# Attention weights of batch 2 through the DMA crossbar, and the second softmax half of batches 4 to 7 one slice earlier

## The chip, the cores and the metric

One core of one Trainium2 chip. The metric is the device time of the whole program in microseconds (us). Small effects are read from the traces, from a fixed matmul on, and the times are a check on the sum.

## The reference

Eight batches of a cross attention between 512 tokens and 32 state rows per head (8 heads of 64), both ways, followed by a gated feed-forward network on the 8 x 544 rows.

```python
def _attn_ref(x, state):                       # x [8,8,512,64], state [8,8,32,64]
    scores = scale * np.matmul(x, state.transpose(0, 1, 3, 2))
    a = np.exp(scores - scores.max(-1, keepdims=True)); a /= a.sum(-1, keepdims=True) + 1e-09
    xread = np.matmul(a, state)
    ...                                        # a2: softmax over the tokens, the other way round
    sread = np.matmul(a2, x)
    return np.concatenate([xread, sread], axis=2)

def _moe_ref(x, w_gate, w_val, w_out):         # [4352,512], 512 -> 1536 -> 512
    return (np.maximum(x @ w_gate, 0.0) * (x @ w_val)) @ w_out
```

## The kernel before

The kernel never forms `xread`. It multiplies each batch's state with the weights once (`U`, matmuls `up`), so that gate and value are `a` times `U` (matmuls `gv_ps<-ans,U`). For that the attention weights `a_sn`, which the softmax leaves with tokens on the partitions, have to be transposed to `ans`. In the kernel before this is done by TensorE for batches 0, 1 and 2, and by the DMA crossbar for batches 3 to 7.

```python
    def att_aT_dma(b):                                   # crossbar
        ans_alloc(b)
        nc.sync.dma_start_transpose(out=ANS[b].rearrange("p k c t -> p (k c) t"),
                                    in_=a_sn[b].rearrange("p k c m -> p (k c m)"))

    def att_T(b, kc):                                    # TensorE: 4 transposes into one PSUM bank
        ...
        for c in range(NC):
            nc.tensor.transpose(ps[:, c], a_sn[b][:, kc, c], id128)
        held["aT", b, kc] = ps

    def att_out(b, kc, eng):                             # and a copy out of PSUM
        copy[eng](out=ANS[b][:, kc], in_=held["aT", b, kc])
```

The part up to batch 2 is a hand-written list of steps (`aT.2.1@4` is `att_T(2, 1)` in PSUM bank 4, `ao` is `att_out`). From there on a loop runs over slices: one slice is a group of four `gv` matmuls, its relu on ScalarE, its product on VectorE, and a group of four `o_ps` matmuls for a slice 18 earlier. Twelve slices make a batch, and work for the next batch is hung on fixed slices:

```python
    for b in range(3, B):
        s = b - 1                                        # work for batch b in the slices of batch b-1
        for i, jf in enumerate((4, 5) if b == 3 else (3, 5)):
            at(s, jf, att_half, b, i)                    # scores, exp (ScalarE), sum, reciprocal, scaling (VectorE)
        for part, jf in enumerate((7, 10)):
            at(s, jf, u_block, b, part)                  # three groups of 8 up matmuls, six PSUM banks
        if b + 1 < B:
            at(s, 9, x_next, b + 1)                      # cast of x on GpSimd, then crossbar transpose xT
            at(s, 9, x_pad, b + 1)                       # copy xa on GpSimd
        if b + 2 < B:
            at(s, 10, x_dma, b + 2, (nc.sync,))          # 1 MB load of x
    for b in range(B):
        s, jf = {0: (2, 3), 1: (2, 4), 2: (2, 7), 3: (2, 10)}.get(b, (b - 1, 10))
        if b > 1:
            at(s, jf, sr, b)
        at(s, jf + 1, sr_T_dma, b)                       # crossbar transpose of sn
        at(s, jf + 6, sr_out, b, "act")                  # copy br on ScalarE, waits for it
    ...
    for g in range(first, NF * (B + 1)):                 # cut
        gv(b, jf); relu(b, jf); mult(b, jf)
        out_piece(...)
        for f in units.get(g, ()):
            f()
```

Six PSUM banks go round among `gv_ps` (two per slice), scores (one) and `up` (two per group). All transfers that the change touches are issued by SyncE, from one queue, in program order.

The softmax here doesn't subtract the row's maximum and nothing guards it: scores larger than these inputs give would overflow.

## Time and profile before

| | kernel before |
|---|---|
| time, median of three runs | 223.29 us (222.69 to 223.47) |
| span of the profiled execution | 221.3 us |
| start of the last store, which ends the chain of waits | 216.40 us |
| start of the up block of batch 4 to the gv group after it | 88.88 - 86.48 = 2.40 us |
| the same for batches 5, 6, 7 | 1.70 to 1.71 us |

An up block is three groups of `up` matmuls followed by four `o_ps` matmuls; the next `gv` start is used as its end, because in some traces the record of the first `o_ps` matmul is missing.

One more view matters: the transfers in SyncE's queue, with start, duration of the issue, and what is moved.

```profile
73.10 1.81 SPq L168 DMA_TRANSPOSE xT<-xb  x1
75.01 1.10 SPq L105 DMA_DIRECT2D xf<-in_x_dram  x1
76.20 0.59 SPq L377 DMA_DIRECT2D out_dram<-o_sb  x1
76.88 1.45 SPq L286 DMA_TRANSPOSE hs_sb<-sn  x1
```

The small transpose of `sn` is issued 1.9 us after a 1 MB load, and lands 1.2 us after it (82.80 and 81.61 us in the trace).

### The profile page before, as it was taken

The page shows a single profiled execution, that of the slowest core. Times are in us where ns is not written, and L with a number is a line of the kernel's source. Part 1 is how long each engine was busy: PE and PEld are TensorE (multiplying, and loading weights), DVE is VectorE, ACT ScalarE, POOL GpSimd, SP SyncE. Part 2 cuts the span into 40 slices and gives each one's busy share as a digit, 9 for nine tenths or more (in the row PEclk, how much of TensorE's full clock was granted, in tenths as well). Part 3 has the DMA queues.
Part 4 walks back from the last instruction along what each step waited for, and adds up shares of the span by engine and source line. Part 5 has one row for each costly group of instructions (what it writes and reads, how often), then busy time and mean ns, then how long its engine had stood idle before and what let it go on. Part 6 is the DMA issues. An engine that isn't in the chain of part 4 may idle for free.

```text
span 221.3 us, 4871 instructions
## 1 busy us (share of the span) xinstructions
PE 216.4 (98%) x1955; PEld 105.9 (48%) x1955; DVE 129.9 (59%) x229; ACT 125.1 (57%) x238; POOL 48.6 (22%) x54
## 2 busy tenths in 40 slices
PE   7899999999999999999999999999999999999994
PEld 3554455444544453444444444445444445666544
DVE  2697898965787558564767378646875333222100
ACT  5599887565667547465565456645654544222222
POOL 8777845460001524006000700000000000000000
PEclk9999999999999999999999999999999999999999
DMA  7999999172058582691169113511311112211132
GB/s 154 174 194 196 199 241 277 49 192 77 16 116 241 110 275 78 141 264 52 49 146 280 58 47 95 110 41 50 96 50 53 49 47 47 52 56 71 66 95 95
DMA packets 40343, 26.01 MB, mean 118 GB/s; under 512 B 21536, under 2 KB 35744, under 8 KB 40320
## 3 DMA queue, kind: packets, MB, share of 16 engines
q1 hardware_dynamic: 27456, 17.47, 28.4%
q0 software_dynamic: 11968, 7.47, 21.9%
q10 hardware_dynamic: 896, 0.75, 1.3%
q8 instruction: 15, 0.25, 0.5%
q14 instruction: 8, 0.07, 0.1%
HBM read 18.35 MB, written 8.91 MB: 123 GB/s over the span
## 4 chain that ended last, share of the span: by engine, by line
PE 88%; DMA 7%; DVE 1%; ACT 1%; POOL 1%; issue 1%; DVEq 0%; POOLq 0%; ACTq 0%
PE o_ps L365 37%; PE gv_ps L328 36%; PE gv_ps L345 5%; PE up L303 4%; DMA xb<-in_x_dram 3%; DMA hs_sb<-sn 3%; PE upc L303 2%; PE sc_ps L209 1%; PE sr_ps L273 1%; DMA out_dram<-o_sb 1%; PE xT_ps L195 1%; PE aT_ps L244 1%; DVE h_sb L356 1%; ACT o_sb L373 1%; POOL xb L427 0%
## 5 line engine op out<-in xcount | busy, mean ns | idle before, releaser
L365 PE MATMUL o_ps<-wo_sb,h_sb 128*128 128x512 bf16 x372 | 94.8, 379 | 0.0
L328 PE MATMUL gv_ps<-ans,U 128*128 128x512 bf16 x384 | 94.0, 379 | 0.0
L356 DVE TENSOR_TENSOR h_sb<-gv_ps,g_sb 128x512 bf16<-128x512 f32 x96 | 65.1, 689 | 44.1 <-ACT g_sb L352 42.2
L352 ACT ACTIVATE g_sb<-gv_ps 128x512 bf16<-128x512 f32 (+1 forms) x108 | 62.5, 581 | 45.2 <-PE gv_ps L328 34.4
L328 PEld LDWEIGHTS <-U 128*128 128x128 bf16 x384 | 36.2, 98 | 42.2 <-issue 0.4
L365 PEld LDWEIGHTS <-h_sb 128*128 128x128 bf16 x372 | 35.2, 98 | 39.7 <-issue 1.6
L373 ACT COPY o_sb<-o_ps 128x512 f32<-128x512 f32 x31 | 18.3, 590 | 17.2 <-PE o_ps L365 17.2
L313 ACT CAST U<-up 128x512 bf16<-128x512 f32 x36 | 19.0, 593 | 11.7 <-PE up L303 11.7
L313 DVE CAST U<-up 128x512 bf16<-128x512 f32 x36 | 22.7, 684 | 4.0 <-PE up L303 3.7
L151 POOL CAST xb<-xf 128x1024 bf16<-128x1024 f32 x10 | 10.1, 1042 | 67.5 <-DMA xf<-in_x_dram 67.5
L265 POOL COPY xa<-xb 128x2048 bf16<-128x2048 bf16 (+1 forms) x9 | 15.2, 1711 | 1.3 <-issue 1.0
L222 DVE TENSOR_REDUCE cs<-e_sn 128x16 f32<-128x512 bf16 x16 | 10.9, 682 | 7.4 <-ACT e_sn L216 7.4
L356 DVE TENSOR_TENSOR hs_sb<-gv_ps,g_sb 128x256 bf16<-128x256 f32 x12 | 5.1, 425 | 15.3 <-PE gv_ps L345 10.1
L216 ACT ACTIVATE e_sn<-sc_ps 128x512 bf16<-128x512 f32 x16 | 9.6, 600 | 7.8 <-PE sc_ps L209 7.7
L228 DVE TENSOR_TENSOR a_sn<-e_sn,rc 128x512 bf16<-128x512 bf16 x16 | 11.7, 736 | 0.4
L303 PEld LDWEIGHTS <-stT 64*32 64x32 bf16 x512 | 6.0, 90 | 10.6 <-issue 9.3
L323 ACT CAST U<-upc 128x512 bf16<-128x512 f32 (+1 forms) x21 | 9.7, 534 | 0.6 <-PE upc L303 0.6
L303 PE MATMUL up<-wg_sb,stT 64*32 64x512 bf16 x144 | 8.0, 382 | 0.2 <-DVE h_sb L356 0.2
L209 PEld LDWEIGHTS <-xT 128*128 128x128 bf16 x128 | 5.9, 99 | 4.1 <-DVE xT L186 0.8
L303 PE MATMUL up<-wv_sb,stT 64*32 64x512 bf16 x144 | 7.6, 380 | 0.0
L345 PE MATMUL gv_ps<-br,wg_sb 128*128 128x256 bf16 x48 | 7.2, 273 | 0.0
L345 PE MATMUL gv_ps<-br,wv_sb 128*128 128x256 bf16 x48 | 7.2, 273 | 0.0
(62 smaller groups left out, 119.4 us busy)
## 6 DMA issues: line engine op xcount, KB each, us to landing
out_dram<-o_sb SPq DMA_DIRECT2D x29, 256.0 KB, 2.3
xf<-in_x_dram SPq DMA_DIRECT2D x4, 1024.0 KB, 6.4
wo_sb<-in_moe_w_out_dram POOLq DMA_DIRECT2D x2, 768.0 KB, 13.4
wg_sb<-in_moe_w_gate_dram POOLq DMA_DIRECT2D x5, 256.0 KB, 8.9
wv_sb<-in_moe_w_val_dram POOLq DMA_DIRECT2D x5, 256.0 KB, 9.5
xf<-in_x_dram POOLq DMA_DIRECT2D x1, 1024.0 KB, 15.0
xb<-in_x_dram POOLq DMA_DIRECT2D x3, 256.0 KB, 6.5
out_dram<-o_sb SPq DMA_DIRECT2D x5, 128.0 KB, 2.3
```

Source lines behind the costliest of these rows:

```text
L151: copy[eng](out=xb[b][:, :, hs].rearrange("p c h d -> p h c d"), in_=xf[b][:, hs])
L222: nc.vector.reduce_sum(out=cs, in_=e_v, axis=AX.X)
L228: {"dve": nc.vector, "pool": nc.gpsimd}[eng].tensor_tensor(out=by_pair(a_sn[b], jp).rearrange("p r (j n) -> p r j n", n=Ns), in0=e_v, in1= ...
L265: nc.gpsimd.tensor_copy(out=v[:, hs:hs + src.shape[1]], in_=src)
L303: nc.tensor.matmul(dst[parity][32 * j:32 * j + 32], stT[r:r + 64, b, j, 32 * parity:32 * parity + 32], wsb[r:r + 64, j, lo:lo + n], start= ...
L313: copy[eng](out=U[b][:, w, kc, lo:lo + 512], in_=held["u", b, w, lo][kc])
L328: nc.tensor.matmul(ps[w], U[b][:, w, kc, f0:f0 + 128], ANS[b][:, kc].rearrange("p c t -> p (c t)"), start=(kc == 0), stop=(kc == NK - 1))
L345: nc.tensor.matmul(ps[w][:, 0:nt], wsb[:, j, f0:f0 + 128], br[:, j].rearrange("p b n -> p (b n)"), start=(j == 0), stop=(j == NJ - 1))
L352: nc.scalar.activation(out=g_sb[:, 0:n], in_=ps[0][:, 0:n], func=AF.Relu)
L356: nc.vector.tensor_tensor(out=dst, in0=ps[1][:, 0:n], in1=held["g", b, jf][:, 0:n], op=ALU.mult)
L365: nc.tensor.matmul(held["o", b, tsub], src[:, jf, tsub * 128:(tsub + 1) * 128], wo_sb[:, jf], start=(jf == 0), stop=(jf == NF - 1))
L373: copy[eng](out=o_sb, in_=held["o", b, tsub])
```

## The change

Three things: batch 2's weights go through the crossbar too (step `ad`), which takes 8 transposes off TensorE and two copies off ScalarE and VectorE; the second softmax half of batches 4 to 7 is hung on slice 4 in place of 5; one store near the end is no longer split in two.

```diff
-        n = 2 if b == B - 2 and tsub < 2 else 1
+        n = 2 if b == B - 2 and tsub < 1 else 1
@@ the list of steps (cut)
-    o.0.3@6 nx.2.1 of.0.0.act u.2.0.1024@05 ...
+    o.0.3@6 nx.2.1 ad.2 of.0.0.act u.2.0.1024@05 ...
-    ... uo.2.0.0.1.dve aT.2.1@4 uo.2.1.512.0.dve o.0.5 ao.2.1.act o.0.6@7 ...
+    ... uo.2.0.0.1.dve uo.2.1.512.0.dve o.0.5 o.0.6@7 ...
-    ... re.1.8 aT.2.0@3 o.0.8 mu.1.8 ao.2.0.dve o.0.9@6 ...
+    ... re.1.8 o.0.8 mu.1.8 o.0.9@6 ...
@@
-        for i, jf in enumerate((4, 5) if b == 3 else (3, 5)):
+        for i, jf in enumerate((4, 5) if b == 3 else (3, 4)):
```

More of the change, by code (lines that the diff above doesn't have):

```diff
@@ L454 @@
              "c": c_unit, "co": c_out, "u": u_unit, "uo": u_out, "gv": gv, "re": relu, "mu": mult, "o": out_part,
-             "of": fin_x, "xn": x_next, "xp": x_pad, "sr": sr_mm, "sn": sr_norm}
+             "of": fin_x, "xn": x_next, "ad": att_aT_dma, "xp": x_pad, "sr": sr_mm, "sn": sr_norm}
     program = """
@@ L476 @@
     mu.1.10 nr.2.0 sc.2.1@5 gv.0.9@34 ex.2.1 re.0.9 nx.2.0 o.0.1 mu.0.9 gv.1.11@12 nr.2.1 xn.3 re.1.11 o.0.2 mu.1.11
-    o.0.3@6 nx.2.1 of.0.0.act u.2.0.1024@05 u.2.1.512@34 uo.2.0.1024.0.dve uo.2.0.1024.1.act sr.0@1 sr.1@2
-    uo.2.1.512.1.act sn.0 u.2.0.0@50 sn.1 xp.2 xp.3 o.0.4 uo.2.0.0.0.act uo.2.0.0.1.dve aT.2.1@4 uo.2.1.512.0.dve
-    o.0.5 ao.2.1.act o.0.6@7 of.0.1.act u.2.1.0@12 u.2.0.512@50 uo.2.1.0.0.act uo.2.1.0.1.dve u.2.1.1024@34 o.0.7
-    uo.2.1.1024.0.act uo.2.1.1024.1.dve uo.2.0.512.0.act gv.1.8@12 uo.2.0.512.1.dve re.1.8 aT.2.0@3 o.0.8 mu.1.8
-    ao.2.0.dve o.0.9@6 of.0.2.act gv.2.0@45 re.2.0 gv.2.2@01 mu.2.0 re.2.2 gv.2.1@23 mu.2.2 re.2.1 gv.2.3@45 mu.2.1
+    o.0.3@6 nx.2.1 ad.2 of.0.0.act u.2.0.1024@05 u.2.1.512@34 uo.2.0.1024.0.dve uo.2.0.1024.1.act sr.0@1 sr.1@2
+    uo.2.1.512.1.act sn.0 u.2.0.0@50 sn.1 xp.2 xp.3 o.0.4 uo.2.0.0.0.act uo.2.0.0.1.dve uo.2.1.512.0.dve
+    o.0.5 o.0.6@7 of.0.1.act u.2.1.0@12 u.2.0.512@50 uo.2.1.0.0.act uo.2.1.0.1.dve u.2.1.1024@34 o.0.7
+    uo.2.1.1024.0.act uo.2.1.1024.1.dve uo.2.0.512.0.act gv.1.8@12 uo.2.0.512.1.dve re.1.8 o.0.8 mu.1.8
+    o.0.9@6 of.0.2.act gv.2.0@45 re.2.0 gv.2.2@01 mu.2.0 re.2.2 gv.2.1@23 mu.2.2 re.2.1 gv.2.3@45 mu.2.1
     re.2.3 mu.2.3
```

## The prediction

> **What bounds the kernel now.** I read the first page first, for the busy shares and the granted clock.
>
> ```profile
> span 221.3 us, 4871 instructions
> ...
> PE 216.4 (98%) x1955; PEld 105.9 (48%) x1955; DVE 129.9 (59%) x229; ACT 125.1 (57%) x238; POOL 48.6 (22%) x54
> ...
> PE   7899999999999999999999999999999999999994
> ...
> PEclk9999999999999999999999999999999999999999
> ```
>
> TensorE is busy from the second slice to the last but one at full clock, the others near 60% or less. But 98% doesn't say that no time is lost, because the ends of matmuls are modelled and overlap: single records of gv_ps and o_ps show 379 ns, while the chain of waits counts four in 0.86 us, 216 ns each. So losses must be looked for in the starts. The chain is nearly all TensorE, except for the startup, the last store and one place between 76 and 88 us:
>
> ```profile
> 76.88 5.92 DMA hs_sb<-sn
> ...
> 82.82 0.02 ACT br L290
> ...
> 86.34 1.29 DVE h_sb L356 x2
> ...
> 87.67 0.41 PE up L303 x7
> 88.08 0.97 PE o_ps L365 x4
> ```
>
> Columns: start, length, what. Here a transfer, then ScalarE, then VectorE set the pace, until a group of up matmuls. The timeline of TensorE says what that cost: the first rows below are this block (the one after batch 4's softmax), the last two the same block one batch later.
>
> ```profile
> 86.48 0.41 PE L303 MATMUL up<-wg_sb,stT 64*32 64x512 bf16 x8
> 86.71 0.77 PE L303 MATMUL up<-wv_sb,stT 64*32 64x512 bf16 x8
> 87.10 0.39 PE L303 MATMUL up<-wg_sb,stT 64*32 64x512 bf16 x1
> 87.67 0.41 PE L303 MATMUL up<-wg_sb,stT 64*32 64x512 bf16 x7 [0.19 <-DVE h_sb L356]
> 88.01 1.04 PE L365 MATMUL o_ps<-wo_sb,h_sb 128*128 128x512 bf16 x4
> ...
> 110.54 0.41 PE L303 MATMUL up<-wg_sb,stT 64*32 64x512 bf16 x8
> ...
> 111.37 1.04 PE L365 MATMUL o_ps<-wo_sb,h_sb 128*128 128x512 bf16 x4
> ```
>
> From the block's first start to the next o_ps start it is 88.01 - 86.48 = 1.53 us against 111.37 - 110.54 = 0.83 us. So 0.70 us is lost here, although the view prints only 0.19 us as idle. The block at 62.76 (0.82 us to the matmuls after it) and that at 133.90 (0.83 us) lose nothing. Past the startup I found no other gap.
>
> **Why that place stalls.** ScalarE works in program order, and just there it waits:
>
> ```profile
> 82.82 0.47 ACT L290 COPY br<-hs_sb 128x128 bf16<-128x128 bf16 x1 [2.29 <-DMA hs_sb<-sn]
> 83.05 0.67 ACT L352 ACTIVATE g_sb<-gv_ps 128x512 bf16<-128x512 f32 x1
> 83.62 0.57 ACT L373 COPY o_sb<-o_ps 128x512 f32<-128x512 f32 x1
> 84.08 0.61 ACT L216 ACTIVATE e_sn<-sc_ps 128x512 bf16<-128x512 f32 x1
> ```
>
> The transposed sn of batch 3 lands 5.9 us after its issue (median of the eight: 2.9), since the 1 MB load of x for batch 5 was issued at 75.01 ahead of it on the same queue. After the 2.29 us the backlog is a relu, an o_sb copy and the exponential of the second half of batch 4; VectorE then does this half's sum, reciprocal and scaling (84.72 to about 86.3), and only then the two products h_sb (86.34 to 87.63) that free the banks up waits for.
>
> **What the Trainium skill says.** "VectorE: DVE Perf Modes", The three transpose paths, gives 390 ns for a 128x128 bf16 transpose on TensorE and 1309 ns on the crossbar. This trace agrees that the crossbar is the slower path per tile (a one-tile sn transpose: median 2.9 us to landing, with the fixed part), but pipelined the TensorE ones cost far less than 390 ns: four in 0.22 us. "TensorE: Matmul & The Clock Gate", Part 4, says that the output of a TensorE transpose goes to PSUM and needs a copy; the trace has these copies (586 ns on ScalarE, 415 ns on VectorE for batch 2). "DMA: Bandwidth & Descriptors", Anatomy of one DMA, says that the issuing sequencer waits for semaphores, not the DMA engines; so a transfer that isn't ready holds back all issues behind it. The trace agrees: at 78.42 a merged issue record of two stores spans 6.12 us, as its second waits for ScalarE.
>
> **Part 1, the transposes of batch 2.** Removed from TensorE:
>
> ```profile
> 45.50 0.22 PE aT_ps L244 x4
> ...
> 50.05 0.22 PE aT_ps L244 x4
> ```
>
> Both groups lie on the chain, between matmuls without a gap: 2 x 0.22 = 0.44 us; the neighbouring starts give 223 ns each, so 0.45 us. The two copies out of PSUM (0.59 us on ScalarE, 0.41 us on VectorE) go as well, but neither engine bounds there: ScalarE idles 0.6 us and VectorE 0.5 us right before them. These count zero.
>
> Added: one crossbar transpose on SyncE's queue. Its input is ready at about 43.5 (scaling starts 41.99, 1.48 us long). It stands behind batch 3's xT transpose:
>
> ```profile
> 42.95 2.11 SPq L168 DMA_TRANSPOSE xT<-xb  x1
> ```
>
> So it issues at about 45.1 and takes 1.25 us of the queue, as the five existing ones of its kind do (landing after 3.0 to 3.1 us). The xT packets occupy the DMA engines to about 47.3, so I estimate its packets from 47.3 to 48.7 and landing at 49 to 50. The first user is the first gv of batch 2: 52.00 in the chain less 0.45 = 51.55. Spare: 1.5 to 2.5 us. The stores behind it shift by some 1.3 us; their copies end at about 42.6, 47.2 and 51.8, and there are four o_sb buffers, so nobody waits.
>
> **Part 2, the second half one slice earlier (batches 4 to 7).** Nothing is added or removed. One o+gv slice is 1.73 us. For batch 4 the second exponential now stands ahead of the blocked br copy, so it runs inside ScalarE's 2.29 us idle time, and VectorE's sum, reciprocal and scaling (0.64 + 0.29 + 0.61 us by starts) run at about 82.3 to 83.9, while it would idle until 83.75. Retracing in times of before: relu of slice 5 at 83.05, its product about 83.9 to 84.5; relu of slice 6 about 84.1, product to 85.4; the matmuls of slice 7 end at about 85.6, its relu to 86.2, its product to 86.9. The third up group starts at 86.93 without a stall. So I count all of the 0.70 us, less at most 0.1.
>
> For batches 5 to 7 there is nothing to gain: their blocks take 0.83 us already. Two halves in consecutive slices ask VectorE for 2 x 2.2 us against 2 x 1.95 us of matmuls, a backlog of 0.5 us; but batch 3 already runs so (scores at 57.02 and 58.98), and its block loses nothing. The earlier ans transposes feed a batch that starts many slices later.
>
> **Part 3**, one store of 256 KB in place of two of 128 KB near the end, saves one 0.34 us issue on a queue that isn't on the path: zero. Sum: 223.29 - 0.45 - 0.70 = 222.14; with a little less of the stall recovered, 222.2 us.
>
> **The rivals.**
> - The crossbar transpose is late, and TensorE waits at the first gv of batch 2. For it: sn of batch 3 landed 3 us late behind a load. Against: here no big load is in flight (the x load before it lands at 40.85). A 2 us slip would eat up the spare; each further us is a us: 223 to 224.
> - The ScalarE block stays and the stall only moves: the sn still lands at about 82.8, and relu of slice 5 still can't run before. Then only the 0.45 us is gained: 222.8. Against it: six banks in rotation let TensorE run three slices ahead, and VectorE's 1.6 us in the way is what used up this slack.
> - The backlog of consecutive halves stalls the gv of batches 5 to 7 by some 0.3 us each: 223. Batch 3 speaks against it.
> - The time saved is absorbed by a load later. Against: after 88 us the chain is TensorE alone up to the last store of 2.06 us.
>
> **Range and chances.** The three runs of before spread over 0.8 us, 222.69 to 223.47, so a new median can lie 0.3 either way; with the partial-recovery case above and some luck below, 221.5 to 222.9. A change of 2% is 4.5 us; nothing that can be removed here is as large, and only a late transfer of 6 us would cost it.
>
> **What would show it.** Right: no aT_ps in the part after 40 us; ans of batch 2 issued near 45 and landed before 51, no wait of TensorE on it; the block of up near 86 takes 0.83 us; ScalarE still waits for sn, but less than 2.29 us, as an exponential fills part of it; TensorE's end moves from the 217th us to about the 216th. Wrong: a gap ahead of gv at 51.5, an up block over 1 us, or new gaps at the scores of batches 5 to 7.

## More of the kernel before

The prediction shows the page, the chain and the timelines, and says how to read them. It doesn't show the gv group after batch 4's block:

```profile
88.88 1.89 PE L328 MATMUL gv_ps<-ans,U 128*128 128x512 bf16 x8
```

## The result, and the profile after

The changed kernel took 221.69 us in the median (221.67 to 221.79, four runs), the kernel before 223.21 us in the four runs of both series. The ratio is 0.9936 (95% interval 0.9917 to 0.9954). A ratio here is the mean time of one kernel's fast runs over that of the other's of the same rounds, so not quite the ratio of the medians. Executions over 1.5% slower than the fastest of the same kernel are left out of the means. The change is worth 0.6%, far below a difference of 2%.

The first page of the changed kernel, the span and the engines' busy time:

```profile
span 219.9 us, 4854 instructions
...
PE 215.0 (98%) x1947; PEld 105.1 (48%) x1947; DVE 130.3 (59%) x228; ACT 124.0 (56%) x237; POOL 49.0 (22%) x54
```

TensorE's share stays at 98%; a share can't show a change of this kind. Its chain of waits does (start, length, what):

```profile
44.49 2.70 PE o_ps L365 x12
...
51.52 4.32 PE gv_ps L328 x20
...
86.84 0.97 PE o_ps L365 x4
```

The `aT_ps` pieces are gone: 12 `o_ps` matmuls now run without a break. Between 76 and 88 us the chain is TensorE alone, without the transfer, ScalarE and VectorE that stood there before. The issue of the new transpose in SyncE's queue, and then the up block of batch 4 and of batch 5 on TensorE:

```profile
45.08 1.65 SPq L236 DMA_TRANSPOSE ans<-a_sn  x1
```

```profile
86.00 0.41 PE L303 MATMUL up<-wg_sb,stT 64*32 64x512 bf16 x8
86.23 0.40 PE L303 MATMUL up<-wv_sb,stT 64*32 64x512 bf16 x8
86.44 0.40 PE L303 MATMUL up<-wg_sb,stT 64*32 64x512 bf16 x8
86.78 1.04 PE L365 MATMUL o_ps<-wo_sb,h_sb 128*128 128x512 bf16 x4
87.65 1.89 PE L328 MATMUL gv_ps<-ans,U 128*128 128x512 bf16 x8
...
109.31 0.41 PE L303 MATMUL up<-wg_sb,stT 64*32 64x512 bf16 x8
...
109.75 0.40 PE L303 MATMUL up<-wg_sb,stT 64*32 64x512 bf16 x8
...
110.95 1.67 PE L328 MATMUL gv_ps<-ans,U 128*128 128x512 bf16 x7
```

The block of batch 4 fell from 2.40 to 87.65 - 86.00 = 1.65 us, that of batch 5 from 1.71 to 1.64. What ScalarE, VectorE and GpSimd do ahead of batch 4's block, from their timelines:

```profile
80.93 0.60 ACT L216 ACTIVATE e_sn<-sc_ps 128x512 bf16<-128x512 f32 x1 [0.88 <-PE sc_ps L209]
82.86 0.47 ACT L290 COPY br<-hs_sb 128x128 bf16<-128x128 bf16 x1 [1.33 <-DMA hs_sb<-sn]
```

```profile
81.81 0.68 DVE L222 TENSOR_REDUCE cs<-e_sn 128x16 f32<-128x512 bf16 x1
82.53 0.25 DVE L224 RECIPROCAL rc<-cs 128x16 f32<-128x16 f32 x1
82.81 1.55 DVE L228 TENSOR_TENSOR a_sn<-e_sn,rc 128x512 bf16<-128x512 bf16 x1
84.28 1.88 DVE L356 TENSOR_TENSOR h_sb<-gv_ps,g_sb 128x512 bf16<-128x512 f32 x3
```

```profile
81.79 2.03 POOL L151 CAST xb<-xf 128x1024 bf16<-128x1024 f32 x2 [6.79 <-PE gv_ps L328]
83.88 2.24 POOL L265 COPY xa<-xb 128x2048 bf16<-128x2048 bf16 x1
```

The exponential now runs ahead of the blocked `br` copy, so ScalarE's wait for `sn` is 1.33 us in place of 2.29, and VectorE's part of the half is over before the products. One thing was not expected: the scaling took 1.55 us in place of the usual 0.69. It started while GpSimd's cast ran, and ended (84.36) 0.54 us after the cast did (81.79 + 2.03 = 83.82). GpSimd's copy behind the cast took 2.24 us in place of 1.90. The runs e5 and e9 come back to this.

Where the 1.41 us at the start of the last store (216.40 to 214.99 in the chains) come from, by the start of the same piece in both chains:

| at | before | changed | gained in this stretch |
|---|---|---|---|
| gv group ahead of the first o_ps group (startup, differs between executions) | 36.36 | 36.26 | 0.10 |
| o_ps after the first up groups of batch 2 | 44.53 | 44.49 | -0.06 |
| first gv of batch 2 (the two groups of transposes gone) | 52.00 | 51.52 | 0.44 |
| o_ps after the up block of batch 4 | 88.08 | 86.84 | 0.76 |
| last store (the up blocks of batches 5, 6 and 7) | 216.40 | 214.99 | 0.17 |

### The profile page after: what moved, and what is told of

Same layout as the page of the kernel before. It is cut to its first block, busy times and chain, and to the rows that moved or that the text cites. A ratio compares the mean times of both kernels' runs of the same rounds, so it can differ in the third digit from the quotient of the medians.

```text
span 219.9 us, 4854 instructions
## 1 busy us (share of the span) xinstructions
PE 215.0 (98%) x1947; PEld 105.1 (48%) x1947; DVE 130.3 (59%) x228; ACT 124.0 (56%) x237; POOL 49.0 (22%) x54
## 4 chain that ended last, share of the span: by engine, by line
PE 94%; DMA 4%; ACT 1%; issue 0%; POOL 0%; DVE 0%; DVEq 0%; POOLq 0%
PE o_ps L365 39%; PE gv_ps L328 38%; PE gv_ps L345 5%; PE up L303 4%; DMA xb<-in_x_dram 3%; PE sc_ps L209 2%; PE upc L303 2%; PE sr_ps L273 1%; PE xT_ps L195 1%; DMA out_dram<-o_sb 1%; PE warm_ps L447 1%; PE aT_ps L244 0%; PE xT_ps L182 0%; ACT o_sb L373 0%; ACT xT L186 0%
## 5 line engine op out<-in xcount | busy, mean ns | idle before, releaser
L352 ACT ACTIVATE g_sb<-gv_ps 128x512 bf16<-128x512 f32 (+1 forms) x108 | 63.2, 591 | 43.4 <-PE gv_ps L328 32.0
L228 DVE TENSOR_TENSOR a_sn<-e_sn,rc 128x512 bf16<-128x512 bf16 x16 | 12.6, 793 | 0.4
L303 PEld LDWEIGHTS <-stT 64*32 64x32 bf16 x512 | 5.5, 90 | 9.0 <-issue 7.6
L303 PE MATMUL up<-wg_sb,stT 64*32 64x512 bf16 x144 | 7.5, 380 | 0.0
```

Of the source, the lines that this page charges most:

```text
L228: {"dve": nc.vector, "pool": nc.gpsimd}[eng].tensor_tensor(out=by_pair(a_sn[b], jp).rearrange("p r (j n) -> p r j n", n=Ns), in0=e_v, in1= ...
L303: nc.tensor.matmul(dst[parity][32 * j:32 * j + 32], stT[r:r + 64, b, j, 32 * parity:32 * parity + 32], wsb[r:r + 64, j, lo:lo + n], start= ...
L352: nc.scalar.activation(out=g_sb[:, 0:n], in_=ps[0][:, 0:n], func=AF.Relu)
```

## The experiments

All gave correct results. The times of before, measured beside them, were 223.27 us (first four runs), 223.07 (next four) and 223.29 (last four). "Block" is the time from the start of batch 4's up block to the next gv group, 2.40 us before and 1.65 changed. The medians are over all executions, the ratios over the fast ones.

| run | median us | ratio to before (95% interval) | block, batch 4 | blocks 5 to 7 |
|---|---|---|---|---|
| e1 crossbar alone | 223.19 | 0.9996 (0.9970 to 1.0022) | 2.19 | 1.70 |
| e2 slices alone | 222.26 | 0.9967 (0.9933 to 1.0002) | 1.65 | 1.65 |
| e3 slices, batch 4 alone | 222.48 | 0.9968 (0.9939 to 0.9996) | 1.65 | 1.70 |
| e4 slices, batches 5 to 7 alone | 222.65 | 0.9992 (0.9955 to 1.0028) | 2.43 | 1.65 |
| e5 br copy of batch 3 later | 223.22 | 1.0013 (0.9977 to 1.0050) | 2.15 | 1.70 |
| e6 changed, br copy ahead of exp | 223.23 | 1.0005 (0.9970 to 1.0040) | 2.75 | 1.65 |
| e7 changed, transpose late | 228.71 | 1.0172 (1.0115 to 1.0228) | 1.65 | 1.65 |
| e8 changed, state by crossbar too | 231.84 | 1.0388 (1.0358 to 1.0418) | not used | |
| e9 before, x load later | 222.42 | 0.9951 (0.9918 to 0.9984) | 1.70 | 2.29 in batch 5 |
| e10 changed, x load later | 221.73 | 0.9921 (0.9888 to 0.9955) | 1.65 | 1.65 |
| e11 changed again | 221.64 | 0.9923 (0.9891 to 0.9955) | 1.65 | 1.65 |
| e12 crossbar alone again | 223.13 | 0.9980 (0.9950 to 1.0011) | 2.79 | 1.70 |

### The parts alone: e1 to e4, and e12

e1 and e12 are the changed kernel with this taken back:

```diff
-        for i, jf in enumerate((4, 5) if b == 3 else (3, 4)):
+        for i, jf in enumerate((4, 5) if b == 3 else (3, 5)):
-        n = 2 if b == B - 2 and tsub < 1 else 1
+        n = 2 if b == B - 2 and tsub < 2 else 1
```

> The kernel before with part 1 alone (batch 2's weights transposed by the crossbar; halves in slices 3 and 5 and the stores as before). Theory (the parts act separately): TensorE's chain gains the 2 x 0.22 us of the transposes and the up block of batch 4 still takes 1.5 us; about 0.45 us less than before, 222.7 to 222.8 if before gives 223.2. Rival (most of the gain is freed ScalarE and VectorE time, or an earlier landing of the sn of batch 3): 1 us or more, and the up block of batch 4 shorter.

e2, e3 and e4 are the kernel before with one of these:

```diff
-        for i, jf in enumerate((4, 5) if b == 3 else (3, 5)):
+        for i, jf in enumerate((4, 5) if b == 3 else (3, 4)):                            # e2
+        for i, jf in enumerate((4, 5) if b == 3 else (3, 4) if b == 4 else (3, 5)):      # e3
+        for i, jf in enumerate((4, 5) if b == 3 else (3, 4) if b > 4 else (3, 5)):       # e4
```

> The kernel before with part 2 alone (second halves of batches 4 to 7 in slice 4). Theory: the up block of batch 4 falls from 1.53 to 0.78 us and the up blocks of batches 5 to 7 from 0.83 to 0.78 us, so 0.75 + 3 x 0.055 = 0.92 us less. Rival (only batch 4's stall matters): 0.75 us, the blocks of batches 5 to 7 stay at 0.83 us.

> Part 2 for batch 4 alone. Theory: 0.75 us less than before, all of it in the up block near 86 us; blocks of batches 5 to 7 at 0.83 us.

> Part 2 for batches 5 to 7 alone. Theory: the stall near 86 us stays (1.5 us), the three later up blocks fall to 0.78 us: 3 x 0.055 = 0.17 us less, below what the times can tell, so it is read from the trace. Rival (my prediction's step, nothing to gain there): 0.83 us in the later blocks as before.

Measured: the slices do what was expected, and separately. In e3 only batch 4's block fell (2.40 to 1.65 us), in e4 only the three later ones (1.70 to 1.65 each), in e2 all four. The rival of e2, that the later blocks have nothing to give, is out; so is that step of the prediction. The times agree in size for e2 and e3, and can't tell e4 from nothing.

The crossbar alone is less clear. It was not measurably faster than before, twice. The times can't settle it: both intervals also hold the 0.998 that a gain of 0.45 us would give. Its first profile lost about 1 us in the startup (TensorE waited for a weight load near 17 us), so it was run again with the changed kernel on one chip:

> Part 1 alone once more: its first profile lost about 1 us in the startup, which hid its gain. Theory: 0.45 us under before in the mean, about 0.9 us above the changed kernel, up block of batch 4 between 1.3 and 1.5 us. Rival (part 1 gives nothing): as before.

> The changed kernel once more, on the same chip as the next run, since the startup differs by up to 1 us between executions and a single chip. About 1.4 us under before by the sum of the trace (0.38 + 0.93 and startup), 130.83 us from the up block of batch 4 to the last matmul.

e11 repeated the first result, 0.9923. In e12 the transposes were gone and TensorE reached the up block at 85.74 rather than 86.48 (0.19 us of this is startup), but there it lost more than before. ScalarE's and TensorE's timelines of e12:

```profile
82.47 0.48 ACT L290 COPY br<-hs_sb 128x128 bf16<-128x128 bf16 x1 [2.68 <-DMA hs_sb<-sn]
```

```profile
85.74 0.41 PE L303 MATMUL up<-wg_sb,stT 64*32 64x512 bf16 x8
...
86.72 0.41 PE L303 MATMUL up<-wv_sb,stT 64*32 64x512 bf16 x7 [0.38 <-DVE h_sb L356]
...
88.53 1.24 PE L328 MATMUL gv_ps<-ans,U 128*128 128x512 bf16 x5
```

The wait for `sn` is longer, as TensorE and so ScalarE are earlier while `sn` isn't by as much, and the block takes 88.53 - 85.74 = 2.79 us. Put beside the other kernels that have the halves in slices 3 and 5 and the br copy in its old place, a rule appears. The first column is the startup, the start of the gv group ahead of the first o_ps group:

| kernel | startup | br copy starts (sn has landed) | up block starts | next gv starts | next gv minus br |
|---|---|---|---|---|---|
| e12 | 36.17 | 82.47 | 85.74 | 88.53 | 6.06 |
| e4 | 36.25 | 82.64 | 86.27 | 88.70 | 6.06 |
| before | 36.36 | 82.82 | 86.48 | 88.88 | 6.06 |
| e1 | 37.33 | 83.11 | 86.98 | 89.17 | 6.06 |

The lines of e1:

```profile
83.11 0.48 ACT L290 COPY br<-hs_sb 128x128 bf16<-128x128 bf16 x1 [2.08 <-DMA hs_sb<-sn]
```

```profile
86.98 0.41 PE L303 MATMUL up<-wg_sb,stT 64*32 64x512 bf16 x8
...
89.17 0.59 PE L328 MATMUL gv_ps<-ans,U 128*128 128x512 bf16 x2
```

In all four, TensorE leaves the block 6.06 us after `sn` lands, whenever it got there. So what TensorE gains ahead of the block is kept only as far as `sn` lands earlier too. The two runs of the crossbar alone differ in this. With the startup taken off, the block is left after 52.52 us before, after 52.36 in e12 and after 51.84 in e1: 0.16 and 0.68 us less, where the transposes are worth 0.45. From there to the last store all three take 127.51 to 127.52 us. So one profile shows most of the gain lost and the other doesn't, and what the crossbar alone is worth stays open.

What differs between the two is the load of x for batch 4: 6.64 us to landing in e12, 6.04 in e1. The crossbar transpose that stands ahead of batch 5's load in the queue waits for the cast of this data, so a late landing delays batch 5's load and `sn` behind it. Over all profiles this load took 5.90 to 6.14 us where its issue took 0.57 us, and 6.64 to 6.85 us where the issue took 1.03 to 1.50. The slow ones are four of the eight profiles with the new transpose and none of the six without it.

The changed kernel's first profile has the slow load, and `sn` landed as late as before (br at 82.86 against 82.82); in its second, e11, the load was fast and br started at 81.95. By the rule above, and as an estimate only, the changed kernel with the old slices would have left the block at 82.86 + 6.06 = 88.92 in the first, no earlier than the kernel before, and at 88.01 in the second. In both profiles it left at 87.5 to 87.7: with the second part it leaves no later than that, with the slow load and with the fast one.

### What holds the block: e5, e6, e9, e10

e5 is the kernel before, with the blocked copy moved out of the way:

```diff
-        at(s, jf + 6, sr_out, b, "act")
+        at(s, jf + (8 if b == 3 else 6), sr_out, b, "act")
```

> The kernel before, with only the br copy of batch 3 (which waits for the transposed sn) two slices later in program order; the halves stay in slices 3 and 5. Theory (the blocked copy on ScalarE is the root of the stall): no wait of ScalarE on sn, the up block near 86 us at 0.83 us as in batch 5, 0.70 us less than before. Rival (VectorE's work of the second half so near the block is what stalls it, with or without the wait): the block keeps more than half of its 0.70 us.

The wait on `sn` was gone, but the block took 2.15 us: of the 0.70 us over the later blocks' 1.70, 0.45 stayed. The rival's number came true, though not for its reason. VectorE and GpSimd in e5:

```profile
85.24 1.14 DVE L228 TENSOR_TENSOR a_sn<-e_sn,rc 128x512 bf16<-128x512 bf16 x1
```

```profile
83.94 1.90 POOL L265 COPY xa<-xb 128x2048 bf16<-128x2048 bf16 x1
```

With the exponential earlier, the scaling met GpSimd's copy, which ended at 85.84, and took 0.45 us more than usual. In the kernel before it had started at 85.73, just after that copy was done (83.76 + 1.90 = 85.66). One wait had been hiding another.

The Trainium skill has the reason, in "SBUF — State Buffer", Who interferes with whom: a VectorE instruction with two SBUF inputs contends with a GpSimd instruction that reads SBUF, and the one that comes second blocks until the first is done. The scaling has two SBUF inputs, and three places agree: 1.55 us in the changed kernel, 1.14 here, and 2.43 in e9 below, each ending 0.54 us after the GpSimd instruction that it met.

e6 is the changed kernel with the order of exponential and br copy turned round in the one slice that they share:

```diff
-        at(s, jf + 6, sr_out, b, "act")
+        if b == 3:
+            units.setdefault(NF * s + jf + 6, []).insert(0, lambda: sr_out(3, "act"))
+        else:
+            at(s, jf + 6, sr_out, b, "act")
```

> The changed kernel, but with the br copy of batch 3 ahead of the second half of batch 4 in the same slice, so that the exponential waits behind the blocked copy. Theory of the prediction (the gain comes from running the exponential inside ScalarE's wait): ScalarE waits 2.3 us again, the exponential runs at about 83.1, the VectorE work of the half at 83.7 to 85.3, and the products come later: the up block loses 0.2 to 0.6 us again. Rival (being a slice earlier is enough, the order against the blocked copy doesn't matter): up block at 0.78 us, time as the changed kernel's.

The block took 2.75 us, more than before the change; the rival (being a slice earlier is enough) is out. The gain comes from the exponential standing ahead of the copy that blocks. The loss is larger than the 0.2 to 0.6 us expected, since the scaling ran into GpSimd's copy as well (started 84.36, 1.57 us long), and all three products came after it. In the changed kernel it was blocked as long, but from 82.81 on, early enough.

e9 is the kernel before with the load of x for batch 5, the source of both waits, issued some 9 us later; e10 is the changed kernel with the same:

```diff
-            at(s, 10, x_dma, b + 2, (nc.sync,))
+            if b == 3:
+                at(3, 5, x_dma, 5, (nc.sync,))
+            else:
+                at(s, 10, x_dma, b + 2, (nc.sync,))
```

> The kernel before, with only the load of x for batch 5 issued about 6 us later, in slice 5 of batch 3; halves in slices 3 and 5, TensorE transposes. It takes away both effects of that load: the transposed sn of batch 3 no longer lands behind it, and GpSimd's cast and copy of batch 5, which block VectorE's scaling, no longer fall at 82 to 86 us. Theory after the run with the later br copy (the stall needs the load: through ScalarE's wait, or with that gone through the blocked scaling): no wait of ScalarE on sn, scaling 0.69 us, the up block at 0.83 us, and 131.06 us or less from this block's start to TensorE's last matmul, against 131.76 before. Rival (the second half in slice 5 is itself too late): the block keeps 0.4 us or more.

> The changed kernel with the same later load. Theory (the changed kernel has no stall left there): the up block stays at 0.78 us, 130.83 us from its start to the last matmul, and the time stays as the changed kernel's. Rival (the load still costs something): faster by 0.1 us or more from 84 us on.

In e9 ScalarE didn't wait for `sn`, the scaling took 0.69 us, and batch 4's block took 1.70 us, like the undisturbed ones before. So the load is the root of batch 4's stall, and slice 5 is not too late in itself, but for the 0.05 us of the later blocks. The stall only moved, though: the next load slid too (issued at 94.70 in place of 92.33), and in the profile batch 5 met it. VectorE and GpSimd there, the first half's scaling:

```profile
104.52 2.43 DVE L228 TENSOR_TENSOR a_sn<-e_sn,rc 128x512 bf16<-128x512 bf16 x1
```

```profile
104.51 1.90 POOL L265 COPY xa<-xb 128x2048 bf16<-128x2048 bf16 x1
```

GpSimd's copy started 0.01 us ahead, and VectorE stood for all of it: batch 5's block took 2.29 us. This time no `sn` was waited for; the blocked scaling alone is enough for a stall. The sum from batch 4's block to TensorE's last matmul fell by only 0.12 us in this profile, where the theory had 0.70. The profiled execution took 223.07 us and the other five 222.06 to 222.59, so it may have been the unluckiest; no trace shows the others. In e10 everything was as in the changed kernel: its halves don't stand where these waits hurt. It is no faster, so there is nothing left to gain from this load.

### How much room the crossbar transpose had: e7 and e8

e7 is the changed kernel with `ad.2` moved from behind `nx.2.1` to behind `of.0.2.act`:

```diff
-    o.0.3@6 nx.2.1 ad.2 of.0.0.act u.2.0.1024@05 ...
+    o.0.3@6 nx.2.1 of.0.0.act u.2.0.1024@05 ...
-    ... mu.1.8 o.0.9@6 of.0.2.act gv.2.0@45 ...
+    ... mu.1.8 o.0.9@6 of.0.2.act ad.2 gv.2.0@45 ...
```

> The changed kernel, with batch 2's crossbar transpose issued after the third o_sb store, some 6.5 us later (about 51.6 instead of 45.1). Theory (the transfer was hidden with under 2 us to spare): landing about 54.7, TensorE waits at the first gv of batch 2 (51.4) for about 3.2 us, time about 224.9, slower than the kernel before. Rival (TensorE isn't held by this transfer, later slack absorbs it): time within 0.5 us of the changed kernel's.

TensorE waited 3.46 us for the transfer, issued at 52.22, at the first gv of batch 2:

```profile
55.52 1.68 PE L328 MATMUL gv_ps<-ans,U 128*128 128x512 bf16 x7 [3.46 <-DMA ans<-a_sn]
```

So the wait is real once the slack is used up. In the changed kernel the trace has the landing at 49.67, and gv starts at 51.36: 1.7 us to spare (1.0 us in e12, where the issue came at 46.93). The time was more than expected: the profiled execution took 225.84 us at a granted clock of 1.000, but the other three took 228.09 to 229.42 at 0.977 to 0.985. Two of these count as slow, so the ratio in the table uses the other two executions of the four, and 1.0172 is only a rough figure.

e8 goes on along the same road: the state of batches 2 and 3 is transposed by the crossbar as well.

```diff
-    ... co.1.1024.256.1.dve stc.1.1.pool
+    ... co.1.1024.256.1.dve stc.1.1.pool stTd.1
-    stc.2.1.pool re.0.11 gv.0.8@64 mu.0.11 re.0.8 stT.1@3 gv.1.10@10 mu.0.8 sto.1.act ...
+    stc.2.1.pool re.0.11 gv.0.8@64 mu.0.11 re.0.8 gv.1.10@10 mu.0.8 stod.1.act ...
```

> The changed kernel, with the state of batches 2 and 3 transposed by the crossbar as well, in place of four transposes on TensorE near 36 us. If the transfer lands in time (before the scores of batch 2 at 37.0; the input is ready at about 32.3): 0.22 us less, 221.5. If it is late, since the wo loads keep the DMA engines busy to 38 us: TensorE waits at the scores, 1 to 3 us slower than the changed kernel.

It takes 0.22 us off TensorE, and the time was 8.8 us over that of before. The transfer's view shows why, and the windows view (stretch, length, busy time of PE, PEld, DVE, ACT and POOL with instructions, granted clock, DMA share, GB/s) what came on top:

```profile
DMA to landing us min/median/max: 2.4/2.4/11.2
```

```profile
44.66 0.59 PE L209 MATMUL sc_ps<-stT,xT 128*128 128x64 bf16 x8 [6.83 <-ACT stT L138]
```

```profile
45.00:47.00 2.00, 2.00 (x14) 0.90 (x12) 1.71 (x4) 0.70 (x2) 1.21 (x2) 0.50 0.03 8
```

Issued at 32.80 beside 2.5 MB of loads that GpSimd had queued, and of which the last landed at 44.14, the transpose landed 11.2 us later. TensorE stood 6.83 us and then ran at half clock for 3.8 us, until 48.5. The Trainium skill warns of this in "TensorE: Matmul & The Clock Gate", Why this matters for your kernels (no idle gaps over some 3 us between bursts of matmuls); the trace agrees for 6.8 us of idle time. After e7's 3.46 us the profiled execution kept the full clock. Its other three had 0.977 to 0.985 in the mean, where no kernel without such a gap fell below 0.992; they have no trace, so that they lost it after the gap is likely but not shown.

## Why the prediction was right, and where it was not

The measured 221.69 us lies in the range of 221.5 to 222.9, 0.5 us below the predicted 222.2.

- The transposes on TensorE: 0.45 us predicted, 0.44 measured between the same matmuls. That the two copies count zero holds as well: no other start moved there but one up group, which lost 0.06 us.
- The crossbar transfer: issue at 45.1, landing at 49 to 50 and 1.5 to 2.5 us to spare were predicted; it was 45.08, 49.67 and 1.7 us. e7 shows that beyond the spare time TensorE waits.
- The stall of batch 4: "all of the 0.70 us, less at most 0.1" became 0.76 us. The mechanism, the exponential inside ScalarE's wait, is shown by e6 and e3. The size was off because the block that served as the yardstick (0.83 us to the next o_ps) itself loses 0.05 to 0.06 us: changed, it takes 0.78.
- The same mistake makes the step that failed: "For batches 5 to 7 there is nothing to gain". Each gained 0.05 to 0.06 us, together 0.17; e4 shows it alone. The timeline had a sign of it: batch 5's third up group takes 0.46 us, against 0.40 in the changed kernel, and the products that free its banks end just as it begins (109.70 + 1.28 = 110.98):

```profile
110.99 0.46 PE L303 MATMUL up<-wg_sb,stT 64*32 64x512 bf16 x8
```

```profile
109.70 1.28 DVE L356 TENSOR_TENSOR h_sb<-gv_ps,g_sb 128x512 bf16<-128x512 f32 x2
```

- VectorE's retraced times (sum to scaling at 82.3 to 83.9) came out at 81.8 to 84.4. The scaling took 1.55 us, not 0.61, since GpSimd's cast wasn't counted. There was just enough room: the products ended at 86.16, 0.28 us before the third up group, which is luck. The kernel before had shown the effect: the scaling of 1.48 us that the prediction quotes at 41.99 ended 0.55 us after a cast of GpSimd. (The sum takes 0.72 us by starts in the lines of before, 84.72 to 85.44, not the 0.64 written.)
- The rival that a load absorbs the time saved was turned down because the chain after 88 us is TensorE alone. That was the wrong place to look: it can be absorbed at 86 us, where the block ends 6.06 us after `sn` lands. With the crossbar alone e12 shows this for most of the 0.45 us, e1 doesn't. The prediction added two separate gains without asking; that it came out is in part luck, as the second part also freed TensorE from the wait for `sn`.
- Of the 0.5 us, the stall (0.76 against the 0.64 that 222.2 allows for), batches 5 to 7 and 0.10 us of startup, less 0.07 us around the transposes, make 0.32; 0.08 is the median of before, which fell with its fourth run. The rest isn't placed.

What stays open: why the load of x for batch 4 is slow in some executions, what the crossbar alone is worth, and what the unprofiled executions of e9 did.

## What to carry to other kernels

When an engine at 98% still waits somewhere, look at what the wait is tied to: if it ends a fixed time after a transfer lands, work saved ahead of it counts only as far as the transfer lands earlier too, until the work behind the transfer is moved. In an in-order engine, put what doesn't need a late transfer ahead of the instruction that waits for it; the order within one slice was worth 1.1 us here (e6 against the changed kernel). Move a transpose to the crossbar only where its input is ready well ahead of its use (here the scaling ended at 43.43, and the transpose landed at 49.67, 6.2 us later) and no big load is in the queues.

## What the Trainium skill lacked or had wrong

- "VectorE: DVE Perf Modes", The three transpose paths, and "TensorE: Matmul & The Clock Gate", Part 4, give 390 ns for a 128x128 transpose on TensorE, the second also about 275 ns in one kernel; neither gives a spacing for several in a row. Here one record is 219 ns long, and four between other matmuls took 0.22 us, 56 ns from start to start; it is this figure that says what a move to the crossbar can save.
- "DMA: Bandwidth & Descriptors" gives no time for a crossbar transpose beside other traffic. Landing took 2.4 us in a quiet queue for a 4-tile transpose of the state and 11.2 us beside 2.5 MB of loads (e8); a one-tile transpose took 2.3 us alone and 5.9 us behind a 1 MB load.
- "SBUF — State Buffer", Who interferes with whom, was right on VectorE's two-input instructions against GpSimd's reads; what it lacks is a time for such a pair. Here 0.69 us became 1.14, 1.55 and 2.43 us, and each time 0.54 us were left to do when GpSimd's instruction ended.
